# Clustered attention and a SoLU block on one core: another order of all queues, and small copies, casts, scalings and products shared otherwise between three engines

## The chip, the cores and the metric

The kernel runs on one core of a Trainium2 chip. The time is that of one execution on the device in microseconds (us); it is given as the median of several runs, and beside it stands one more execution that was taken with the hardware profiler. The engines are TensorE (PE in the profile, its weight loads PEld), VectorE (DVE), ScalarE (ACT), GpSimd (POOL) and SyncE (SP, which issues most DMAs). Each engine works through its own queue in the order in which its instructions were written, and waits at an instruction until what it needs is there.

## The reference

Attention for 4 batches, 8 heads, 768 tokens and 64 columns, in which a query sees the keys of its own cluster alone (16 clusters for each head, chosen by the greatest product with a normalised centroid), and behind it a block with two weights over the 3072 tokens:

```python
q_assign = np.argmax(np.einsum('bhsd,hcd->bhsc', q_n, c_n), axis=-1)
k_assign = np.argmax(np.einsum('bhsd,hcd->bhsc', k_n, c_n), axis=-1)
scores = np.where(q_assign[..., :, None] == k_assign[..., None, :], scale * q @ k.T, -1e9)
attn = softmax(scores) @ v
x = attn.transpose(0, 2, 1, 3).reshape(B * S, H * D)      # 3072 x 512
h = x @ w_in                                              # 3072 x 1024
solu = h * softmax(h)
ln = (solu - mean) / sqrt(var + 1e-6) * g_ln
out = ln @ w_out                                          # 3072 x 512
```

## The kernel before, in words

The work is cut into named steps. A step is written with `add(name, engine, ..., fn, needs, after)`; its function emits the instructions. What sets the order is a list written out by hand or by a program, `ORDER`: `Weave.run` goes through it and calls one function after the other, so each engine's queue is the list's steps of that engine in the list's order. `AWAY` names the steps that run on another engine than their default. A step's numbers are batch, pair of heads, and so on.

*Loads and clusters.* `ld` and `lv` load q, k and v for a pair of heads. In the first batch PE turns the tokens (`tp`, L396), and two copies to SBUF take them up: `xa` and `xt` (L407 on ACT, L409 on DVE). In the later batches DVE turns them (`xt`, L421). `ca` casts them to bf16 into `qbig` and `kbig` (L437 on ACT, L439 and L441 on DVE or POOL); `cv` casts v (L554 on ACT, L556 on the others). `cl` are the products with the centroids (L470), which `cx`, `cy`, `cz`, `cp` and `cb` have normalised, turned and written into `g_wide` (`cb` is L934). Then DVE turns the result back (`tb`, L479), takes the maximum (`mx`, L489), compares (`oh`, L493) and turns the one-hot rows (`ot`, L505 or L500). `pl` copies them below the casted q and k (L529 on ACT, L531 on the others), so that the product of the scores holds the mask; `bl` clears unused rows.

*Attention.* `S` are scores (L641), in regions of 1024 columns; four banks, `sb0` and `sb1`, hold two regions in turn. `E` is the exponential of a region on ACT (L651, 144 of them), which can start when both its halves are there, and frees the region for the scores two further on. `V` are the products with v (L663) into the one bank `ob`; `N` (L675, L686) divides by the sum on DVE and frees `ob` for the next group. In the first batch the heads come in the order of the pairs: pair 0 has the first nine regions, pairs 1 to 3 three each.

*The block.* `tx` turns x by DMA; `h` is the product with w_in (L774) into the banks `hb0` and `hb1`; `hm` (L784, DVE) brings it to SBUF and takes the maximum; `ex` (L800, ACT) is the exponential; `u` the product of both (L807, POOL or DVE); `tu` turns u by DMA (the last two by PE, L761, and a copy); `bn`, `ag` and `as` (DVE, POOL) and `al` (L842, POOL) make the variance and the factor alpha; `y` is the product with w_out (L846); `sc` scales it by alpha (L859 on ACT, L861 on DVE) and `ou` writes it out. There are 24 blocks of 128 tokens. Up to the 21st all y go through the one bank `mb`, so y of a block starts when `sc` of the block before has read the bank. `ce` (L618 on DVE, L622 and L624 on POOL) centres w_out once, `wi` casts w_in.

So the choice of an engine is made by lines such as these, and nothing else in the steps knows of it:

```python
def on(name, engine):
    return AWAY.get(name, engine)
...
e = on(f"sc{f}", "ACT")
```

## Time and profile before

| | us |
|---|---|
| median of 3 runs | 222.06 |
| the three runs | 222.46, 222.06, 220.9 |
| the profiled execution | 221.02 |
| its span, first to last instruction | 219.2 |
| busy: PE, ACT, DVE, POOL | 211.8, 193.0, 185.0, 159.0 |

The profile's page gives an engine's busy time as a share of the span; a share near one says that the engine is worth a look, not that it is the bound everywhere. The stages (a table of stretches of time) tell where each engine is full. In the groups of instructions the last columns are the busy time, the mean of one in ns, and the idle time of the engine just before them with what ended it. In a timeline each row has its start, its duration, the engine, the line and the operation.

### The profile page before, as it was taken

What the parts mean: (1) busy time and instruction counts of PE and PEld (TensorE: products, weight loads), DVE (VectorE), ACT (ScalarE), POOL (GpSimd) and SP (SyncE); (2) the same over time, 40 slices, a digit from 0 to 9 for tenths busy, and PEclk for the clock granted to TensorE, in tenths of its full rate; (3) what the DMA queues carried; (4) which work ended last, traced back from release to release, by engine and by line L of the source; (5) the groups of instructions that cost most, each with busy time, mean ns of one, the idle gap of its engine ahead of it and who ended that gap; (6) DMA issues with size and microseconds to landing.
All of it is one profiled execution on the core that took longest, in us unless ns stands there. A gap on an engine that the chain in (4) does not pass through costs nothing.

```text
span 219.2 us, 6308 instructions
## 1 busy us (share of the span) xinstructions
PE 211.8 (97%) x2429; PEld 148.0 (68%) x2429; DVE 185.0 (84%) x429; ACT 193.0 (88%) x246; POOL 159.0 (73%) x198
## 2 busy tenths in 40 slices
PE   7799999999999999999999999999999999999993
PEld 3467477677678776777677677666677766755552
DVE  3699978978999999896899999994888756889893
ACT  4699999999999998999999989999999888785472
POOL 4586969987898999549939987979969154555530
PEclk9999999999999999999999999999999999999999
DMA  6999999999799992998989973939484329695614
GB/s 198 372 403 299 180 182 301 150 155 274 134 189 175 164 185 45 174 250 174 190 211 173 180 155 63 178 96 215 133 162 101 93 48 171 138 151 132 185 60 156
DMA packets 120910, 38.33 MB, mean 175 GB/s; under 512 B 109992, under 2 KB 116400, under 8 KB 120880
## 3 DMA queue, kind: packets, MB, share of 16 engines
q1 hardware_dynamic: 120448, 37.40, 81.1%
q10 hardware_dynamic: 432, 0.52, 0.7%
q8 instruction: 19, 0.31, 0.6%
q14 instruction: 11, 0.09, 0.2%
HBM read 23.11 MB, written 6.29 MB: 134 GB/s over the span
## 4 chain that ended last, share of the span: by engine, by line
PE 74%; ACT 10%; DVE 9%; issue 2%; DMA 2%; POOL 0%; SPq 0%; DVEq 0%
PE sb L641 22%; PE hb L774 17%; PE mb L846 15%; PE ob L663 12%; ACT e L651 7%; PE hb L470 3%; DMA raw<-in_k_dram 2%; DVE w_st L784 2%; DVE xt L421 2%; DVE bs L818 2%; PE hb L846 2%; ACT xt L407 1%; PE hb L396 1%; DVE x L686 1%; ACT v L554 1%
## 5 line engine op out<-in xcount | busy, mean ns | idle before, releaser
L651 ACT ACTIVATE e<-sb 128x1024 bf16<-128x1024 f32 x144 | 139.8, 1023 | 8.7 <-PE sb L641 7.9
L641 PE MATMUL sb<-qbig,kbig 80*128 80x256 bf16 (+3 forms) x648 | 83.7, 261 | 1.1 <-ACT e L651 1.0
L641 PEld LDWEIGHTS <-kbig 80*128 80x128 bf16 (+1 forms) x648 | 62.9, 119 | 25.5 <-issue 8.8
L807 POOL TENSOR_TENSOR u<-e_sb,w_st 128x1024 bf16<-128x1024 bf16 x21 | 45.0, 2144 | 19.3 <-ACT e_sb L800 13.1
L663 PEld LDWEIGHTS <-e 128*128 128x128 bf16 x1152 | 48.6, 97 | 10.4 <-DVE x L686 0.6
L774 PE MATMUL hb<-w_in_sb,xT 128*128 128x512 bf16 x192 | 53.4, 379 | 0.0
L663 PE MATMUL ob<-v,e 128*128 128x65 bf16 x1140 | 51.4, 193 | 0.0
L846 PE MATMUL mb<-w_out_c,uT 128*128 128x512 bf16 x168 | 45.6, 379 | 0.4 <-DVE y L861 0.4
L818 DVE BATCH_NORM_STATS2 bs<-u 128x6 f32<-128x512 bf16 x48 | 31.9, 681 | 1.1 <-POOL u L807 1.1
L800 ACT ACTIVATE e_sb<-w_st,nmax 128x1024 bf16<-128x1024 f32 (+1 forms) x25 | 27.8, 1113 | 5.5 <-DVE w_st L784 4.1
L441 POOL TENSOR_SCALAR kbig<-xt 64x768 bf16<-64x768 f32 (+1 forms) x32 | 28.4, 890 | 2.3 <-DVE xt L409 0.7
L439 POOL CAST qbig<-xt 64x768 bf16<-64x768 f32 (+1 forms) x31 | 25.0, 807 | 5.9 <-PE ob L663 2.7
L842 POOL TENSOR_TENSOR alpha<-var,halves 128x1 f32<-128x1 f32 x24 | 15.4, 643 | 11.7 <-DVE var L825 11.0
L421 DVE STREAM_TRANSPOSE xt<-raw 128x768 f32<-128x768 f32 x24 | 22.5, 959 | 0.1
L846 PEld LDWEIGHTS <-uT 128*128 128x128 bf16 x176 | 15.1, 97 | 9.8 <-issue 0.5
L774 PEld LDWEIGHTS <-xT 128*128 128x128 bf16 x192 | 15.8, 98 | 8.3
L686 DVE TENSOR_TENSOR x<-ob,den 128x256 bf16<-128x256 f32 (+2 forms) x40 | 19.0, 474 | 1.4
L784 DVE TENSOR_SCALAR_CACHE_REDUCE w_st<-hb 128x512 f32<-128x512 f32 x24 | 16.3, 681 | 4.0 <-PE hb L774 3.9
L784 DVE TENSOR_SCALAR_CACHE_REDUCE w_st<-hb,nmax 128x512 f32<-128x512 f32 x24 | 17.8, 742 | 2.1 <-PE hb L774 1.5
L675 DVE RECIPROCAL den<-ob 128x4 f32<-128x4 f32 (+2 forms) x40 | 7.1, 179 | 10.7 <-PE ob L663 10.4
L556 POOL CAST v<-vf 128x384 bf16<-128x384 f32 x22 | 11.7, 542 | 4.2 <-DMA vf<-in_v_dram 3.6
L531 POOL COPY kbig<-oht 32x768 f32<-32x768 f32 (+2 forms) x14 | 9.9, 711 | 3.2 <-DVE oht L505 1.3
(112 smaller groups left out, 201.4 us busy)
## 6 DMA issues: line engine op xcount, KB each, us to landing
vf<-in_v_dram SPq DMA_DIRECT2D x16, 384.0 KB, 5.7
out_dram<-y SPq DMA_DIRECT2D x20, 256.0 KB, 2.7
raw<-in_k_dram SPq DMA_DIRECT2D x26, 192.0 KB, 4.4
raw<-in_q_dram SPq DMA_DIRECT2D x24, 192.0 KB, 5.3
w_g<-in_moe_w_out_dram SPq DMA_DIRECT2D x4, 512.0 KB, 8.6
w_st<-in_moe_w_in_dram SPq DMA_DIRECT2D x4, 512.0 KB, 7.1
raw<-in_q_dram SPq DMA_DIRECT2D x3, 384.0 KB, 6.5
raw<-in_k_dram SPq DMA_DIRECT2D x3, 384.0 KB, 7.6
```

The lines of the kernel that those rows point to most:

```text
L421: nc.vector.transpose(xts[b, p, i][:], raw_of(b, p, i))
L439: (nc.vector if e == "DVE" else nc.gpsimd).tensor_copy(dst, src)
L441: (nc.vector if e == "DVE" else nc.gpsimd).tensor_scalar(dst, src, scalar1=inv_C, scalar2=1.0, op0=Alu.mult, op1=Alu.mult)
L641: nc.tensor.matmul(reg[:, c:c + wd], kb[u, pp, side_of(h), keys], qb[u, pp, side_of(h), su * P:su * P + wd])
L651: nc.scalar.activation(es[r][:, :w], src, Act.Exp, scale=exp_scale, bias=-exp_scale)
L663: nc.tensor.matmul(ops_of(group_of[n])[:, s, :VW], es[r][:, c0:c0 + P], v1[index[b, pair_of(h)] % R][:, side_of(h), kt, :VW], start=(kt == ...
L774: nc.tensor.matmul(hb[f2][:], xTs[f][:, dc, :], w_in_sb[:, dc, f2 * BANK:(f2 + 1) * BANK], start=(dc == 0), stop=(dc == n_dc - 1))
L784: nc.vector.tensor_scalar(ff[f, "h"][:, f2 * BANK:(f2 + 1) * BANK], hb[f2][:], scalar1=-1.0, scalar2=nmax[:, f2 - 1:f2] if f2 else 3.0e38, ...
L800: nc.scalar.activation(ff[f, "e"][:, cols(f, f2)], ff[f, "h"][:, cols(f, f2)], Act.Exp, bias=ff[f, "nmax"][:, n_ff2 - 1:], scale=-1.0, acc ...
L807: (nc.vector if e == "DVE" else nc.gpsimd).tensor_tensor(ff[f, "u"][:, cols(f, f2)], ff[f, "e"][:, cols(f, f2)], ff[f, "h"][:, cols(f, f2) ...
L818: nc.vector.bn_stats(ff[f, "bs"][:, f2, :], ff[f, "u"][:, f2 * BANK:(f2 + 1) * BANK])
L846: nc.tensor.matmul(y_of(f, x), ff[f, "uT"][:, fc, :], w_out_c[:, fc, parts_of(f, x)], start=(fc == 0), stop=(fc == n_fc - 1))
```

## The change

The two tables are exchanged: `ORDER` as a whole, and `AWAY`. The steps, their instructions and their conditions stay. The diff shows the whole of `AWAY`; of `ORDER` the first line stands for the rest.

```diff
 AWAY = {}
 AWAY.update(dict.fromkeys("""
-    tu22.1 ca0.0.1.1.0 ca0.2.0.1 ca1.0.0.1 ca3.1.1.0 ca3.2.0.1 cv0.0.1 cv0.1.0 cv0.2.1 cv1.2.0
-    cv1.3.1 cv2.0.1 cv2.1.0 cv3.0.0 cv3.0.1 cv3.3.0 pl0.0.0.1 pl0.0.1.0 pl0.1.1.1 pl2.2.1.0
-    xa0.0.0 xa0.1.0 xa0.1.1 xa0.2.0 xa0.2.1 xa0.3.0 xt0.1.0 xt0.1.1 xt0.2.0 xt0.3.0
+    cv0.1.0 cv1.0.1 cv1.2.0 cv2.2.1 pl0.0.0.0 pl0.0.1.0.0 pl3.2.1.1 tu22.1 xa0.0.1 xa0.1.0 xa0.1.1
+    xa0.2.0 xt0.1.0 xt0.1.1 xt0.2.0 xt0.2.1
 """.split(), "ACT"))
 AWAY.update(dict.fromkeys("""
-    as0 as11 as14 as15 as17 as18 as19 as2 as22 as23 as4 as5 as9 bl1.2 bl3.0 ce0 ce2 ce4 km mk
-    pl0.0.1.0.0 pl0.1.0.0 pl0.1.0.1 pl0.2.0.0 pl0.2.1.0 pl0.3.0.0 pl0.3.1.1 pl1.0.0.0
-    pl1.2.0.0 pl2.0.0.0 pl2.0.0.1 pl2.0.1.1 pl2.2.0.0 pl3.0.0.1 pl3.2.0.1 pl3.2.1.0 sc0 sc1
-    sc12 sc13 sc14 sc16 sc4 sc9
+    as1 as10 as14 as16 as18 as2 as20 as21 as22 as23 as3 as4 as7 bl2.0 ca0.0.1.0.0 ca0.2.1.1
+    ca0.3.0.0 ce0 ce2 ce4 cv0.0.0 km mk pl0.0.1.1.0 pl0.2.1.1 pl0.3.0.0 pl0.3.0.1 pl0.3.1.0
+    pl1.0.0.0 pl1.2.0.0 pl2.0.0.0 pl2.2.0.0 pl3.2.0.1 sc0 sc1 sc10 sc11 sc12 sc16 sc2 sc20 sc22 sc3
+    sc4 sc5 sc6 sc8 sc9 xt0.0.0
 """.split(), "DVE"))
 AWAY.update(dict.fromkeys("""
-    ca0.0.0.0.0 ca0.0.0.0.1 ca0.0.0.1.0 ca0.0.0.1.1 ce1 ce3 pl0.0.1.1 u0.0 u1.0 u10.0 u11.0
-    u12.0 u13.0 u15.0 u16.0 u17.0 u18.0 u19.0 u2.0 u21.0 u22.0 u3.0 u4.0 u5.0 u6.0 u7.0 u8.0
-    u9.0
+    ca0.0.0.0.0 ca0.0.0.1.0 ca0.0.0.1.1 ce3 pl0.0.0.1 pl0.0.1.0.1 pl0.0.1.1.1 u0.0 u1.0 u10.0 u11.0
+    u13.0 u14.0 u15.0 u16.0 u17.0 u18.0 u2.0 u20.0 u21.0 u22.0 u23.0 u23.1 u3.0 u4.0 u5.0 u6.0 u7.0
+    u8.0 u9.0
 """.split(), "POOL"))
...
 ORDER = """
-lc ld0.0.0.0 ld0.0.1.0 ld0.0.0 ld0.0.1 ld0.1.0 ld0.1.1 lv0.0 ld0.2.0 ld0.2.1 ld0.3.0 lo3 lv0.1
+lc cx ld0.0.0.0 cy cz wu tp0.0.0.0 ld0.0.1.0 ld0.0.0 tp0.0.0.1 cp xa0.0.0 ld0.0.1 ld0.1.0 tp0.0.1.0
...
```

Counted over the program, ACT gives up seven `sc`, six `cv`, four `ca`, one `pl` and three copies of the first batch. DVE gets seven `sc` (15 in all), one `cv`, three `ca`, three copies of the first batch, one `ce`, and gives up seven `pl` and the two halves of the last `u`. POOL gets eight `pl`, five `cv` and those two halves. The changed kernel is two lines shorter, so its lines have numbers that are lower by two.

Three places of the queues follow. The first is ACT from its fifth exponential to the twelfth (before) and from the first to the tenth (changed): L651 and L649 are the exponentials, the other rows are copies and casts that stand between them. Before:

```order
L651 ACTIVATE e_370<-sb0_90 128x1024
L651 ACTIVATE e_372<-sb1_91 128x1024
L651 ACTIVATE e_427<-sb0_90 128x1024
L651 ACTIVATE e_429<-sb1_91 128x1024
L554 CAST v1_1_103<-vf_157 128x6x64
L529 COPY kbig0_99<-oht_374 32x384
L651 ACTIVATE e_482<-sb0_90 128x1024
L651 ACTIVATE e_484<-sb1_91 128x1024
L437 ACTIVATE qbig1_97<-xt_277 64x6x128
L651 ACTIVATE e_519<-sb0_90 128x1024
L554 CAST v1_2_104<-vf_161 128x6x64
L651 ACTIVATE e_526<-sb1_91 128x1024
```

Changed:

```order
L649 ACTIVATE e_278<-sb0_90 128x1024
L405 COPY xt_289<-hb1_93 128x384
L649 ACTIVATE e_306<-sb1_91 128x1024
L649 ACTIVATE e_314<-sb0_90 128x1024
L649 ACTIVATE e_337<-sb1_91 128x1024
L649 ACTIVATE e_375<-sb0_90 128x1024
L649 ACTIVATE e_396<-sb1_91 128x1024
L649 ACTIVATE e_403<-sb0_90 128x1024
L649 ACTIVATE e_436<-sb1_91 128x1024
L649 ACTIVATE e_453<-sb0_90 128x1024
L552 CAST v1_1_103<-vf_304 128x6x64
L649 ACTIVATE e_480<-sb1_91 128x1024
```

A copy and a cast are left between the exponentials of the first batch's start; the row of q's cast (L437), the one-hot copy (L529) and the second cast of v are on other engines now. Behind the last row shown the changed queue has exponentials alone until past the 21st.

The second place is DVE at the start, from the write of the centroids on (`cst` is the turned-back product, `oh` and `oht` the one-hot rows). Before:

```order
L409 COPY xt_195<-ob_94 128x3x2x64
L934 TENSOR_TENSOR g_wide_113<-mb_95,upper_136 128x256
L479 STREAM_TRANSPOSE cst_208<-mb_95 128x192
L489 TENSOR_REDUCE mx_210<-cst_208 128x12
L493 TENSOR_TENSOR oh_212<-cst_208,mx_210 128x192
L505 STREAM_TRANSPOSE oht_214<-oh_212 128x3x64 x2
L479 STREAM_TRANSPOSE cst_255<-mb_95 128x192
L489 TENSOR_REDUCE mx_257<-cst_255 128x12
```

Changed:

```order
L407 COPY xt_166<-hb0_92 128x3x2x64
L407 COPY xt_166<-hb1_93 128x3x2x64
L932 TENSOR_TENSOR g_wide_113<-mb_95,upper_136 128x256
L439 TENSOR_SCALAR kbig0_99<-xt_186 64x2x3x64
L477 STREAM_TRANSPOSE cst_201<-mb_95 128x192
L487 TENSOR_REDUCE mx_211<-cst_201 128x12
L491 TENSOR_TENSOR oh_214<-cst_201,mx_211 128x192
L477 STREAM_TRANSPOSE cst_222<-mb_95 128x192
L487 TENSOR_REDUCE mx_225<-cst_222 128x12
L503 STREAM_TRANSPOSE oht_227<-oh_214 128x3x64 x2
```

DVE has q's two copies and one cast of k more there, and the second half's turn and maximum stand before the first half's one-hot turn. On PE, at the same time, the turn of the next pair's tokens that stood before the first cluster products stands behind them.

The third place is DVE late in the program, around the scalings of y (`y<-mb,alpha`). Before:

```order
L818 BN_STATS bs_3352<-u_3322 128x6
L675 RECIPROCAL den_3354<-ob_94 128x4
L686 TENSOR_TENSOR x_2909<-ob_94,den_3354 128x256
L784 TENSOR_SCALAR w_st_3357,nmax_3358<-hb0_92 128x512
L861 TENSOR_SCALAR y_3368<-mb_95,alpha_3366 128x512
L818 BN_STATS bs_3352<-u_3322 128x6
L675 RECIPROCAL den_3435<-ob_94 128x4
L686 TENSOR_TENSOR x_2909<-ob_94,den_3435 128x256
L784 TENSOR_SCALAR w_st_3357,nmax_3358<-hb1_93,nmax_3358 128x512
L861 TENSOR_SCALAR y_3479<-mb_95,alpha_3433 128x512
```

Changed:

```order
L859 TENSOR_SCALAR y_3327<-mb_95,alpha_3096 128x512
L782 TENSOR_SCALAR w_st_3370,nmax_3371<-hb0_92 128x512
L782 TENSOR_SCALAR w_st_3370,nmax_3371<-hb1_93,nmax_3371 128x512
L821 BN_AGGR mv_3378<-bs_3184 128x2
L823 TENSOR_SCALAR var_3380<-es6_3314,esum_3055,mv_3378 128x1
L816 BN_STATS bs_3384<-u_3144 128x6 x2
L821 BN_AGGR mv_3410<-bs_3384 128x2
L823 TENSOR_SCALAR var_3412<-es6_3367,esum_3066,mv_3410 128x1
L835 TENSOR_SCALAR es6_3414<-esum_3204 128x1
L859 TENSOR_SCALAR y_3442<-mb_95,alpha_3168 128x512
L816 BN_STATS bs_3461<-u_3250 128x6
```

Between two scalings there stand now two maxima and two statistics in a row, and the scalings of the ninth to thirteenth blocks are all on DVE, as are seven before them.

More of the change, by code (lines that the diff above doesn't have):

```diff
@@ new lines @@
+xt0.1.1 pl0.0.0.0 oh0.0.1 pl0.0.1.0 ot0.0.1 pl0.0.1.1 pl0.0.0.1 tp0.2.0.0 tp0.2.0.1 xa0.2.0
+pl0.0.1.0.1 cl0.1 cv0.0.1 ld1.0.0.0 xt0.2.0 pl0.0.1.0.0 ca0.0.0.1.1 pl0.0.1.1.1 ca0.1.0.0 S0.0 S0.1
+ca0.1.1.0 tp0.2.1.0 ca0.2.0.0 pl0.0.1.1.0 E0 tp0.2.1.1 S1.0 ca0.2.0.1 tb0.1 cv0.0.0 xa0.2.1 S1.1
+tp0.3.0.0 ca0.1.0.1 S2.0 S2.1 mx0.1 xt0.2.1 lv0.1 E1 cl0.2 S3.0 E2 oh0.1 S3.1 V0.0 xa0.3.0
+ca0.2.1.0 lo2 tp0.3.0.1 S4.0 S4.1 E3 ld1.0.0.1 V0.1 lo3 ot0.1 tp0.3.1.0 z1 ca0.1.1.1 S5.0 tb0.2
+S5.1 lv0.2 pl0.1.1.0 V1.0 mx0.2 gt pl0.1.0.1 xt0.3.0 E4 oh0.2 xa0.3.1 V1.1 S6.0 S6.1 N0 gk E5
@@ L142 @@
+ag23 ptu23.1 tu23.1 al23 y22.2 y22.3 tu23.0 sc21 y23.0.0 y23.1.0 ou20 y23.1.1 sc22 ou21 y23.1.2
+y23.1.3 ou22 y23.0.1 y23.0.2 y23.0.3 sc23.1 sc23.0 ou23.1 ou23.0
 """.split()
```

195 lines of the change are left out of this document (93 added, 102 removed).

## The prediction

> **What bounds the kernel now.** I read the page first, then the stages, then the chain of waits, then the groups of one stage at a time. The page's busy times, and its shares of the chain that ended last:
>
> ```profile
> PE 211.8 (97%) x2429; PEld 148.0 (68%) x2429; DVE 185.0 (84%) x429; ACT 193.0 (88%) x246; POOL 159.0 (73%) x198
> PE 74%; ACT 10%; DVE 9%; issue 2%; DMA 2%; POOL 0%; SPq 0%; DVEq 0%
> ```
>
> TensorE (PE) is busy nearly always and is three quarters of the chain. That is an average, and the stages differ. The columns here are the stretch and its length, then the busy time of PE, PE's weight loads, VectorE (DVE), ScalarE (ACT) and GpSimd (POOL):
>
> ```profile
> 0.00:12.20 12.20, 9.55 (x63) 5.03 (x64) 6.57 (x25) 7.14 (x15) 6.46 (x26) 1.00 0.86 297
> 12.20:35.40 23.20, 22.10 (x286) 16.06 (x285) 20.10 (x45) 22.80 (x29) 18.37 (x30) 1.00 1.02 256
> 35.40:60.00 24.60, 24.60 (x334) 17.62 (x331) 22.32 (x46) 24.26 (x28) 21.26 (x25) 1.00 0.96 198
> ```
>
> From 35 us on PE has no idle time; from 12.2 to 35.4 ACT is busy 22.80 of 23.20 us. The chain of waits names the exponentials (L651) in that stage, one each 0.9 us, from 28.36 to 33.79 without a break:
>
> ```profile
> 28.36 0.81 ACT e L651
> 29.26 0.82 ACT e L651
> ...
> 33.79 1.09 ACT e L651
> ```
>
> How much PE can still win later is told by the groups of 35.4 to 216 us (busy, mean ns of one, then idle before):
>
> ```profile
> L641 PE MATMUL sb<-qbig,kbig 80*128 80x256 bf16 (+3 forms) x562 | 71.1, 259 | 0.0
> L846 PE MATMUL mb<-w_out_c,uT 128*128 128x512 bf16 x168 | 45.6, 379 | 0.4 <-DVE y L861 0.4
> ```
>
> One wait of 0.4 us in 180. So there are three stages: a start of 12 us (a chain of small steps), 23 us bound by ACT, and 180 us bound by PE, whose products stay what they are. Work taken off ACT can pay in the second stage alone; in the third the change can hardly win, and can lose.
>
> **Start.** The rows on the way to the first scores (L641) and the first exponential:
>
> ```profile
> 6.88 0.42 DVE L934 TENSOR_TENSOR g_wide<-mb,upper 128x256 f32<-128x256 f32 x1 [0.77 <-PE mb L931]
> 7.28 0.52 PE L396 MATMUL hb<-ident_f,raw 128*128 128x128 f32 x3 [0.44 <-ACT xt L407]
> 7.73 0.53 PE L470 MATMUL mb<-xt,g_wide 128*32 128x192 f32 x8
> 8.33 0.38 DVE L479 STREAM_TRANSPOSE cst<-mb 128x192 f32<-128x192 f32 x1 [1.02 <-PE mb L470]
> 9.53 0.64 DVE L505 STREAM_TRANSPOSE oht<-oh 128x192 bf16<-128x192 bf16 x2
> 11.45 0.35 ACT L529 COPY kbig<-oht 32x192 f32<-32x192 f32 x1
> 12.25 0.60 PE L641 MATMUL sb<-qbig,kbig 80*128 80x256 bf16 x4
> 12.89 1.02 ACT L651 ACTIVATE e<-sb 128x1024 bf16<-128x1024 f32 x1
> ```
>
> In the old order a turn of tokens (7.28) stands before the first cluster products (7.73). In the new one the products come first and can start when L934 has written the centroids, at about 7.1: two copies now stand before it on DVE, which idled 0.77 us there. That is 0.6 us sooner, so the turn back (8.33) comes at 7.7. Then DVE's own steps: turn, maximum and comparison of the first half 1.2 (8.33 to 9.53); turn and maximum of the second, now before L505, two thirds of that, 0.8; L505 0.64; comparison and L505 of the second half 0.4 + 0.64; one copy, 0.35 as at 11.45. The last one-hot rows lie at 11.6 to 11.8, which is where they are now (11.45 + 0.35), but PE was then behind them by 0.45 and a turn of tokens has left that place. First exponential 0.3 to 0.6 us sooner; I take 0.5.
>
> **ACT up to the 21st exponential.** ACT's groups of 12.2 to 35.4 us:
>
> ```profile
> L651 ACT ACTIVATE e<-sb 128x1024 bf16<-128x1024 f32 x21 | 20.1, 1038 | 0.1
> L407 ACT COPY xt<-hb 128x384 f32<-128x384 f32 x4 | 1.9, 484 | 0.2 <-PE hb L396 0.2
> L554 ACT CAST v<-vf 128x384 bf16<-128x384 f32 x2 | 1.0, 511 | 0.0
> L437 ACT ACTIVATE qbig<-xt 64x768 bf16<-64x768 f32 x1 | 0.8, 842 | 0.0
> L529 ACT COPY kbig<-oht 32x384 f32<-32x384 f32 x1 | 0.5, 507 | 0.0
> ```
>
> Two of the four L407 stand before the first exponential. Behind it: 2 x 0.48 + 2 x 0.51 + 0.84 + 0.51 = 3.3 us that are no exponentials. The new queue has one L407 and one L554 there, 1.0 us. That is 2.3 us less, some 0.1 of it in ends that overlap the next start; I take 2.2. With the start, 2.7 us.
>
> **What DVE and POOL take over.** DVE was busy 20.10 of those 23.20 us. It now has two more copies like L409, a cast of v, two casts of tokens and one more L618 there, and a turn of the next batch's tokens (L421) stands earlier; two 32x192 and two 32x384 copies leave it. The rows:
>
> ```profile
> L409 DVE COPY xt<-hb 128x384 f32<-128x384 f32 x3 | 1.6, 550 | 0.1
> L531 DVE COPY qbig<-oht 32x384 f32<-32x384 f32 x4 | 2.2, 558 | 0.1
> L531 DVE COPY qbig<-oht 32x192 f32<-32x192 f32 x2 | 0.9, 452 | 0.0
> L618 DVE SCALAR_TENSOR_TENSOR w_out_c<-w_g,g_ln,y 128x512 bf16<-128x512 f32 x2 | 1.9, 934 | 0.0
> L421 DVE STREAM_TRANSPOSE xt<-raw 128x768 f32<-128x768 f32 x1 | 1.0, 967 | 0.0
> L439 POOL CAST qbig<-xt 64x768 bf16<-64x768 f32 x27 | 23.0, 852 | 5.0 <-PE ob L663 2.7 <-PE sb L641 1.1 <-ACT xt L407 0.4
> ```
>
> A cast of this kind on DVE is in no row: its bounds are the 32x192 copy (0.45) and POOL's cast (0.85). I take 0.6, nearer to the copies of the same engine. Sum: 2 x 0.55 + 3 x 0.6 + 0.9 + 1.0 - 2 x 0.45 - 2 x 0.56 = 2.8 us more, in a stage that is to become 2.7 us shorter: 22.9 us of work for 20.5. All of that does not fit. DVE's normalisations free the bank `ob`; the values that wait for it hold PE's queue, and with it the scores behind them. How much of the 2.4 us is only the overlap of one instruction's end with the next one's start, these rows don't tell; if none of it is, 0.3 us of the gain is left, and if two thirds are, 1.9. At the upper end the casts cost 0.45 each and all 2.7 passes. Between ends so far apart I take **1.9**, since the row it rests on (L651 in a full queue: 1.04 us long, one each 0.9) shows such an overlap of a seventh. POOL was idle 4.8 us in the stage; it gets three copies and loses two casts there: nothing.
>
> ```profile
> 48.82 1.16 DVE L531 COPY qbig<-oht 32x768 f32<-32x768 f32 x1
> 42.56 2.54 POOL L441 TENSOR_SCALAR kbig<-xt 64x768 bf16<-64x768 f32 x2
> ```
>
> These are copies and casts that took far longer than others of their kind: 1.16 where the 32x384 copy takes 0.56, and 1.27 each where POOL's cast takes 0.85. Both engines were at work in both places. The Trainium skill has a rule that speaks against the change here: the GPSIMD Engine Reference, 1. Specifications, says that GpSimd shares its SBUF interfaces with VectorE and contends with Vector instructions in a 2-port mode or with two SBUF inputs. By it the work moved off ACT, which is not named there, would slow both of the others (the second rival); by the group means, which have such rows in them already, it is priced above.
>
> **PE's 180 us.** ACT gives seven scalings of y to DVE: no gain, since ACT is not the limit. The possible loss is in the order. y goes through one bank, `mb`, so y of the next block of tokens waits for the scaling of this one:
>
> ```profile
> 85.60 0.59 PE L846 MATMUL mb<-w_out_c,uT 128*128 128x512 bf16 x2 [0.35 <-DVE y L861]
> 199.56 0.60 PE L846 MATMUL mb<-w_out_c,uT 128*128 128x512 bf16 x2
> 200.30 0.67 ACT L859 ACTIVATE y<-mb,alpha 128x512 f32<-128x512 f32 x1
> 41.96 0.86 PE hb L774 x4
> 43.36 0.55 PE ob L663 x18
> 43.91 0.44 PE sb L641 x4
> ```
>
> From the start of a y's last pair of products to the end of its scaling are 1.41 us (199.56 to 200.97); 0.43 of it is PE's own (half of L774's 0.86), so some 1.0 us of other products must lie between one y and the next. Counted by the last three rows (0.43 for a pair at L774, 0.18 for six at L663, 0.22 for two at L641), the old order leaves at least 1.1; the new one leaves 0.9 to 1.3 at eight places after the ninth y, three of them scaled on DVE. Each may lose nothing, or 0.4 as at 85.60: 0 to 3.2 us. I take **0.5**.
>
> **The end.** Both halves of the last u go from DVE to POOL:
>
> ```profile
> 210.22 1.34 DVE L807 TENSOR_TENSOR u<-e_sb,w_st 128x512 bf16<-128x512 bf16 x2
> 212.48 0.61 PE L761 MATMUL sb<-ident_b,u 128*128 128x128 bf16 x8
> 206.27 2.14 POOL L807 TENSOR_TENSOR u<-e_sb,w_st 128x1024 bf16<-128x1024 bf16 x1 [1.74 <-issue]
> ```
>
> On POOL the two halves take the 2.14 of a whole one, until 212.36 instead of 211.56. Their turn by PE starts at 212.48, behind products of the two blocks before, which are the cover; without it the step costs 0.8. I take 0.
>
> **Sum.** -1.9 + 0.5 = -1.4 us. The profiled execution took 221.02 us (span 219.2), so 219.6 by its measure; the median of the three runs is 222.06, 1.04 above it, so 220.7 by that one. I name the middle, **220.1**.
>
> **Rivals.** 1: DVE has room, and no y waits. For it: two thirds of DVE's excess may be overlap, and closer pairs of y (1.1) cost nothing at 199.56. All 2.7 pay: 218.3 by the profiled run, 218.8 by the middle. 2: DVE takes ACT's place as the bound of the first 35 us, with POOL's contention. For it: 22.9 us of work for 20.5, and five moved copies that lose 0.6 as at 48.82 would add 3.0. Against: DVE's mean for such a copy, 0.56, says that few do. Time: no change, 221.0 to 222.1. 3, slower: DVE's scalings hold PE in the stage where PE is the bound. Fifteen now go through DVE's queue; where one finds a single instruction of 0.7 ahead of it, the bank is late by as much. With three that late the 1.9 is gone; with eight, 5.6 - 1.9 = +3.7, so 224.7 by the profiled run. For it: 85.60. Against: eight scalings were DVE's already, and one of them shows a wait. 4: the order changes nothing because PE is the bound throughout; against it stands the second stage's row.
>
> **How the numbers follow.** My sum has 0.38, rival 1 0.30, rivals 2 and 4 together 0.17, rival 3 0.15. About 1% (2.2 us) is what a measurement of this kernel can tell from no change; the three runs shown lie 0.7% apart. Nearly all of rival 1 and three tenths of my own case (a better cap, no loss at y) are past it: faster 0.40. The rest of mine with rivals 2 and 4: same 0.45. Slower 0.15. The range reaches from all 2.7 with 1.3 us of further waits won in the first 35 us (217.0) to rival 3 with four late scalings beside the median (222.06 + 2.8 - 1.9 = 223.0).
>
> **What would show it.** Right: the first exponential at 12.3 to 12.6 us; the 21st at 32.7 to 33.5 instead of 34.9 (33.79 + 1.09); DVE idle under 1.5 us in the second stage; then PE without idle to the end but for single waits of its y products for DVE's scalings. Wrong: the 21st exponential after 34.5 (DVE or contention took the place), more than 2 us of waits of PE for scalings, or PE waiting for the last u.

## The result, and the profile after

The change makes the kernel slower: 230.05 and 230.34 us, beside 220.72 to 222.46 for the kernel before on the same chip, a ratio of 1.038 with a 95% interval of 1.033 to 1.044. (Two more executions, 234.06 and 948.26 us, fell in a disturbed state and are left out.) The prediction said 220.1, with a range to 223.0; it was wrong in sign. The profiled execution took 230.05 us with a span of 228.2, so 9.0 us more span than before (219.2). The page, its busy times and its chain:

```profile
PE 214.8 (94%) x2399; PEld 147.9 (65%) x2429; DVE 192.3 (84%) x434; ACT 183.4 (80%) x225; POOL 167.5 (73%) x213
PE 58%; DVE 16%; POOL 14%; issue 6%; ACT 4%; DMA 1%; POOLq 0%; DVEq 0%; ACTq 0%
```

ACT gave up 9.6 us of work, as the change says, DVE took up 7.3 and POOL 8.5. The chain tells more: PE's share went from 74% to 58%, and POOL, which was not on the chain at all, has 14%, DVE 16% instead of 9%. The second of the stages shown for the kernel before, and a later stretch:

```profile
12.20:35.40 23.20, 21.85 (x280) 14.74 (x273) 22.09 (x47) 20.40 (x25) 19.55 (x36) 1.00 1.05 249
140.00:170.00 30.00, 26.79 (x316) 18.82 (x318) 24.74 (x52) 24.51 (x30) 25.52 (x30) 1.00 0.39 84
```

The later stretch in the kernel before:

```profile
140.00:170.00 30.00, 30.00 (x329) 21.14 (x324) 24.36 (x59) 28.77 (x39) 25.54 (x28) 1.00 0.73 137
```

In the second stage ACT is no longer full (20.40 of 23.20, was 22.80), and DVE is (22.09, was 20.10). From 140 to 170 us PE, which had no idle time, idles 3.2 us. What it waited for, over the whole changed kernel (line waited for, us in total, times, longest):

```profile
PE hb L772 <- DVE w_st L782: 2.0, 1, 2.0
PE ob L661 <- DVE x L684: 1.8, 2, 1.0
...
PE sb L844 <- DVE w_g L766: 1.1, 1, 1.1
```

Four waits, 4.9 us, all for DVE and none for a scaling of y (one of 1.2 us at the very start, left out here, is in both kernels). They end at 70, 156, 161 and 223 us, and the chain of waits goes through DVE ahead of each. DVE from 147 to 161 us, in the order of its queue, with rows left out:

```profile
147.76 0.56 DVE L684 TENSOR_TENSOR x<-ob,den 128x384 bf16<-128x384 f32 x1
148.23 2.75 DVE L491 TENSOR_TENSOR oh<-cst,mx 128x768 bf16<-128x768 f32 x1
...
155.44 0.56 DVE L684 TENSOR_TENSOR x<-ob,den 128x384 bf16<-128x384 f32 x1
...
156.63 3.07 DVE L529 COPY qbig<-oht 32x768 f32<-32x768 f32 x1
...
160.38 0.74 DVE L782 TENSOR_SCALAR_CACHE_REDUCE w_st<-hb,nmax 128x512 f32<-128x512 f32 x1
```

and POOL at the same time:

```profile
148.03 2.13 POOL L805 TENSOR_TENSOR u<-e_sb,w_st 128x1024 bf16<-128x1024 bf16 x1
...
156.35 0.82 POOL L439 TENSOR_SCALAR kbig<-xt 64x768 bf16<-64x768 f32 x1
157.15 2.13 POOL L805 TENSOR_TENSOR u<-e_sb,w_st 128x1024 bf16<-128x1024 bf16 x1
```

A comparison that takes 0.95 us elsewhere took 2.75: it began 0.20 us behind a u and ended at 150.98, 0.82 us behind u's end (150.16). A one-hot copy took 3.07 us beside a cast and the next u, and ended 0.42 us behind that u. The normalisation at 155.44 and the maximum at 160.38 stood behind these two in DVE's queue, and PE's `V` and `h` waited for them. At 64 and 219 us the same is seen, again a u on POOL beside a comparison, and beside the sum of the two halves' totals (`as` of the last block):

```profile
65.51 2.29 DVE L491 TENSOR_TENSOR oh<-cst,mx 128x768 bf16<-128x768 f32 x1
...
219.69 1.08 DVE L832 TENSOR_TENSOR es<-esum 128x1 f32<-128x1 f32 x1
```

```profile
64.52 2.46 POOL L805 TENSOR_TENSOR u<-e_sb,w_st 128x1024 bf16<-128x1024 bf16 x1
...
218.48 2.28 POOL L805 TENSOR_TENSOR u<-e_sb,w_st 128x512 bf16<-128x512 bf16 x2 [0.91 <-POOL alpha L840]
```

The view of one line's forms gives the spread (duration in ns: least, median, most), after:

```profile
L491 DVE TENSOR_TENSOR oh<-cst,mx x11: 317/950/2747, 8.9 to 148.2; 128x768 bf16<-128x768 f32 x6, 128x384 bf16<-128x384 f32 x3, 128x192 bf16<-128x192 f32 x2
```

and before:

```profile
L493 DVE TENSOR_TENSOR oh<-cst,mx x11: 359/948/1553, 9.1 to 146.9; 128x768 bf16<-128x768 f32 x6, 128x384 bf16<-128x384 f32 x3, 128x192 bf16<-128x192 f32 x2
L834 DVE TENSOR_TENSOR es<-esum x1: 143/143/143, 213.2 to 213.2; 128x1 f32<-128x1 f32 x1
```

Laid beside POOL's rows one by one, no comparison, no SBUF copy and no such sum of DVE ran beside a u in the kernel before. In the changed one five did that became longer by it: 1.3 (65.51), 0.4 (90.01), 1.8 (148.23), 2.5 (156.63; 0.55 elsewhere) and 0.9 us (219.69), some 7 us of DVE in all. Against this stands what the kernel before lost already: six of its comparisons and copies stood beside casts or copies on POOL (at 23.49, 48.82, 62.10, 87.08, 90.71 and 128.96) and were 0.4 to 0.7 us longer each, 3.4 us in all. So meetings are not new; new in the change is that they are with u, and so longer. DVE's statistics, maxima, turns, scalings and normalisations ran beside u dozens of times in both, with no change of length.

The first 36 us cost the rest that has a clear place. The first exponential started at 13.40 instead of 12.89, and the 20th ended at 36.18 instead of 34.88. (The prediction called that row the 21st; it is the 20th.) In the kernel before, the chain of waits of this stage went through ACT, from one exponential to the next. In the changed one it goes through POOL's queue alone, from 14.47 to 31.88 us:

```profile
14.47 0.25 POOL qbig L437
...
31.36 0.51 POOL kbig L529
...
31.92 0.41 PE sb L639 x2
```

Scores stood there behind casts and one-hot copies of POOL, and ACT waited for scores (2.6 us in six waits).

### The profile page after: what moved, and what is told of

Read it like the earlier page. It is cut to its first block, busy times and chain, and to the rows that moved or that the text cites. A ratio compares the mean times of both kernels' runs of the same rounds, so it can differ in the third digit from the quotient of the medians.

```text
span 228.2 us, 6282 instructions
## 1 busy us (share of the span) xinstructions
PE 214.8 (94%) x2399; PEld 147.9 (65%) x2429; DVE 192.3 (84%) x434; ACT 183.4 (80%) x225; POOL 167.5 (73%) x213
## 4 chain that ended last, share of the span: by engine, by line
PE 58%; DVE 16%; POOL 14%; issue 6%; ACT 4%; DMA 1%; POOLq 0%; DVEq 0%; ACTq 0%
PE sb L639 17%; PE mb L844 12%; PE hb L772 12%; PE ob L661 9%; ACT e L649 4%; PE hb L468 3%; POOL qbig L437 3%; DVE oh L491 3%; POOL kbig L439 3%; DVE bs L816 2%; DVE w_st L782 2%; POOL kbig L529 2%; POOL u L805 2%; POOL qbig L529 2%; POOL v L554 1%
## 5 line engine op out<-in xcount | busy, mean ns | idle before, releaser
L649 ACT ACTIVATE e<-sb 128x1024 bf16<-128x1024 f32 x144 | 141.1, 1022 | 21.9 <-PE sb L639 20.8
L639 PE MATMUL sb<-qbig,kbig 80*128 80x256 bf16 (+3 forms) x648 | 94.4, 263 | 2.2 <-ACT e L649 0.9
L639 PEld LDWEIGHTS <-kbig 80*128 80x128 bf16 (+1 forms) x648 | 61.4, 121 | 29.8 <-issue 10.4
L805 POOL TENSOR_TENSOR u<-e_sb,w_st 128x1024 bf16<-128x1024 bf16 (+1 forms) x23 | 47.6, 2071 | 24.3 <-DMA uT<-u 14.2
L661 PEld LDWEIGHTS <-e 128*128 128x128 bf16 x1152 | 50.4, 97 | 14.4 <-DVE x L684 3.9
L661 PE MATMUL ob<-v,e 128*128 128x65 bf16 x1140 | 54.2, 194 | 2.1 <-DVE x L684 1.8
L772 PE MATMUL hb<-w_in_sb,xT 128*128 128x512 bf16 x175 | 51.3, 379 | 2.6 <-DVE w_st L782 2.0
L844 PE MATMUL mb<-w_out_c,uT 128*128 128x512 bf16 x156 | 43.0, 379 | 0.4
L437 POOL CAST qbig<-xt 64x768 bf16<-64x768 f32 (+1 forms) x32 | 26.7, 839 | 2.9 <-DVE xt L407 1.8
L529 POOL COPY kbig<-oht 32x768 f32<-32x768 f32 (+2 forms) x17 | 13.1, 768 | 11.0 <-DVE oht L498 7.8
L554 POOL CAST v<-vf 128x384 bf16<-128x384 f32 x27 | 13.5, 515 | 0.7
```

Source lines behind the costliest of these rows:

```text
L437: (nc.vector if e == "DVE" else nc.gpsimd).tensor_copy(dst, src)
L639: nc.tensor.matmul(reg[:, c:c + wd], kb[u, pp, side_of(h), keys], qb[u, pp, side_of(h), su * P:su * P + wd])
L649: nc.scalar.activation(es[r][:, :w], src, Act.Exp, scale=exp_scale, bias=-exp_scale)
L661: nc.tensor.matmul(ops_of(group_of[n])[:, s, :VW], es[r][:, c0:c0 + P], v1[index[b, pair_of(h)] % R][:, side_of(h), kt, :VW], start=(kt == ...
L772: nc.tensor.matmul(hb[f2][:], xTs[f][:, dc, :], w_in_sb[:, dc, f2 * BANK:(f2 + 1) * BANK], start=(dc == 0), stop=(dc == n_dc - 1))
L805: (nc.vector if e == "DVE" else nc.gpsimd).tensor_tensor(ff[f, "u"][:, cols(f, f2)], ff[f, "e"][:, cols(f, f2)], ff[f, "h"][:, cols(f, f2) ...
```

## The experiments

The theory after the traces: (a) DVE's instructions with two operands in SBUF, and its copies from SBUF to SBUF, wait for the end of a POOL instruction that is under way; (b) in the first batch POOL's queue took ACT's place. The rivals: the moved work is the loss wherever it stands; or DVE is late by its order and the long rows fill time in which it would wait anyway. Each kernel's lines have the numbers of the kernel before. Medians in us and ratios to the kernel before:

| kernel | median | ratio, 95% interval |
|---|---|---|
| old order, new sharing | 252.4 | 1.139, 1.132 to 1.146 |
| new order, old sharing | 241.0 | 1.083, 1.074 to 1.092 |
| first 36 us old | 230.2 | 1.039, 1.033 to 1.045 |
| three steps off the meetings | 227.0 | 1.026, 1.020 to 1.031 |
| and POOL relieved in the first batch | 225.7 | 1.020, 1.016 to 1.024 |
| two u later | 228.3 | 1.030, 1.026 to 1.035 |
| before, last u on POOL | 221.5 | 1.001, 0.997 to 1.004 |
| all edits together | 225.1 | 1.015, 1.011 to 1.020 |
| the same, PE's holes filled | 224.7 | 1.012, 1.010 to 1.015 |
| new start, old rest | 222.8 | 1.007, 1.004 to 1.009 |
| new until 143 us, old end | 228.1 | 1.032, 1.028 to 1.035 |
| old until 145 us, new end | 231.8 | 1.048, 1.043 to 1.053 |

**Order and sharing apart.**

```diff
-ORDER of the change, AWAY of the change
+ORDER of the kernel before, AWAY of the change
```

> The old order with the new sharing between the engines. The theory: the new kernel loses its 9 us in two ways, in POOL's full queue in the first 36 us (some 1.5 us) and, for the larger part, where a comparison, an SBUF copy or the small sum of two numbers on VectorE stands beside a product u on GpSimd and waits for its end (2.75 us instead of 0.95, 3.07 instead of 0.65, 2.29 instead of 0.95, 1.08 instead of about 0.14). Which of these meet u depends on the order and on who makes u; with the old order the comparisons meet u at no place unless the moved u (the 14th-, 20th- and 23rd-block ones on GpSimd now) do, so I expect 223 to 226: the last u on GpSimd costs about 1 us, the rest a little. Rival: the moved work itself (scalings to VectorE, copies to GpSimd) is the loss whatever the order, then 228 to 231.

```diff
-ORDER of the change, AWAY of the change
+ORDER of the change, AWAY of the kernel before
```

> The new order with the old sharing. The theory: the meetings of comparisons and copies on VectorE with u on GpSimd at 65, 148 and 157 us come from the order and stay, the end (last u back on VectorE) is as before, and POOL's queue in the first 36 us is lighter: 225 to 229, with single waits of TensorE over 1 us for VectorE between 140 and 170 us. Rival (the moved work is the loss): 221 to 223.

Both missed by far, 252.4 and 241.0 us. An order that was made for one sharing is a bad order for the other: in the first, PE waits 4.3 us for maxima on DVE, 2.4 for POOL's one-hot copies, 2.1 for a scaling and 2.0 for a cast. So these two don't divide the 9 us, and nothing follows on the rival.

**The first 36 us old.**

```diff
-ORDER and AWAY of the change
+ORDER and AWAY of the kernel before up to the scores of region 21, of the change behind
```

> The changed kernel whose first part, until the scores of the 22nd region (some 36 us), has the old order and the old sharing; behind it all is as in the change. The theory: the first part is worth the time by which the 20th exponential came later (36.18 against 34.88 us) and perhaps a little more behind it, so 1 to 2 us less than the change: 228.0 to 229.3. Rival: the first part loses all (late by 1.3 us there, and everything behind it falls into worse meetings): under 225. Other rival: the later stages have slack for it, no change, 230.

230.2 us: no change. That is the time of the second rival, by which the later stages have slack; the theory missed. The trace doesn't settle it. Its first exponential started at 13.23 and the 20th ended at 35.59, so 0.6 us were won there, in spite of a new wait of 0.7 us for a load of w_out at 23 us; a second new wait, of 0.6 us for a normalisation at 36.8, stands at the seam, where eight steps of the new order are added, and took as much back. The four runs lie between 228.9 and 231.5, so one us can't be told here. The comparison of 2.74 and the copy of 3.07 us stand as in the change.

**Three steps off the meetings.**

```diff
 AWAY of the change, with
-u10.0 on POOL, pl3.2.0.1 and as23 on DVE
+u10.0 on DVE, pl3.2.0.1 on ACT, as23 on POOL
```

> The changed kernel with three steps on another engine: the product u of the eleventh block on VectorE instead of GpSimd (it stood beside the comparison that took 2.75 us), one copy of one-hot rows (the one that took 3.07 us beside the next u) on ScalarE instead of VectorE, and the two small operations of the last block's variance (1.08 us beside the last u, 0.14 elsewhere) on GpSimd instead of VectorE. The theory: TensorE's waits of 1.13 and 2.19 us at 156 and 161 us and most of the 1.22 us at 223 us go, so 225.5 to 227. Rival: VectorE's queue is late there because of its order, and the two long rows only fill time in which it would wait anyway: then 229 to 231, the waits of 1 to 2 us stay.

227.0 us, at the upper end of the theory's range and 3.2 us less than the change; the rival's 229 to 231 is out. DVE did not get less work of its own by it: u takes 1.22 us there, the copy and the sum that left take 0.55 and 0.14 by themselves. PE's waits:

```profile
PE ob L663 <- DVE x L686: 1.8, 2, 0.9
...
PE sb L846 <- DVE w_g L768: 0.5, 1, 0.5
```

The 2.0 us for the maximum are gone, the 1.1 at the end are 0.5. The wait for the normalisation at 155 us stayed (0.9): u itself on DVE now fills 1.22 us of the same queue. The two profiled executions differ by 4.1 us (230.05 and 225.98). PE's waits are 2.6 us of that; another 1.3 us are the start, whose first exponential came at 12.11 instead of 13.40 although nothing was edited there. So a part of the 3.2 us between the medians may be the start too.

**POOL relieved in the first batch.** The kernel just shown, and

```diff
-ca0.2.0.1, pl0.1.1.1, cv0.2.1 on POOL
+ca0.2.0.1, pl0.1.1.1, cv0.2.1 on ACT
```

> As the kernel with three steps moved (the one that took 226.97 us), and three more of the first batch go from GpSimd to ScalarE: one cast of q, one copy of one-hot rows and one cast of v, which were ScalarE's in the kernel before. The theory: behind the first exponential the changed kernel was bound by GpSimd's queue (no idle time from 12.9 to 32.9 us), since the 20th exponential ended 22.8 us after the start of the first one, against 22.0 before. With 1.9 us less on GpSimd that stretch becomes 21.3 to 22.0 us, and the time 0.7 to 1.5 us less: 225.5 to 226.3. Rival: ScalarE is the bound there after all; then the three steps make it 22.8 us or longer and the time stays at 227 or rises.

225.7 us, a time within the theory's range. But it is 0.5% below the kernel just shown (ratios of 1.020 and 1.026, measured on two chips), and the two intervals overlap. Twenty us from the first exponential on, in the kernel before, in the change and here:

```profile
12.89:32.89 20.00, 19.17 (x242) 13.50 (x241) 17.48 (x40) 19.83 (x26) 15.37 (x25) 1.00 1.02 252
```

```profile
13.40:33.40 20.00, 18.97 (x241) 12.79 (x240) 19.02 (x40) 17.53 (x20) 18.15 (x33) 1.00 1.06 231
```

```profile
11.89:31.89 20.00, 19.44 (x244) 13.30 (x243) 19.23 (x40) 19.31 (x23) 16.09 (x30) 1.00 1.08 252
```

In the change ACT (the fourth engine, 17.53) has 2.5 us to spare, and POOL (the fifth) has 33 instructions instead of 25, 2.8 us more. With three of them back on ACT, PE gets 0.5 us more done in the 20. The stretch from the first exponential to the end of the 20th, however, fell only from 22.78 to 22.43 us, not to 22.0: by then PE, DVE and ACT are all near full. What the trace does show is the place of the bound: with these three steps back on ACT the chain of waits from the first exponential to the 20th has no piece of POOL any more, it goes through PE and ACT.

**The last u alone**, in the kernel before:

```diff
-u23.0 u23.1 on DVE
+u23.0 u23.1 on POOL
```

> The kernel before with one edit: both halves of the last block's u on GpSimd instead of VectorE, as in the change. The theory: the small sum on VectorE that stands behind them in the queue waits for the second half's end, its row becomes 0.8 us or more longer, the last copy of turned u comes later, and TensorE waits 0.6 to 1.2 us for it before the last products: 0.6 to 1.2 us more than before, 221.9 to 222.5. My prediction (products of the two blocks before cover it): no change.

No change, 221.5 us: the theory's 0.6 to 1.2 us missed, and the prediction's "0" for that edit was right in the old order. There a statistic stands ahead of the small sum on DVE, which meets only the rest of u:

```profile
211.49 0.69 DVE L818 BATCH_NORM_STATS2 bs<-u 128x6 f32<-128x512 bf16 x1 [0.64 <-POOL u L807]
212.10 0.50 DVE L834 TENSOR_TENSOR es<-esum 128x1 f32<-128x1 f32 x1
```

So u on POOL is not enough for the 1.1 us at the end of the change; the sum right behind its start belongs to it (with that sum on POOL, three steps moved, the wait was 0.5).

**The meeting by itself.** Behind the last step of the kernel before, five kinds of DVE instruction run alone and behind the start of POOL's instructions; nothing else is at work. `step` is a tiny operation on one number for each row, by which one engine waits for the other; `hot`, `copy`, `small`, `stats` and `turned` are the comparison, the one-hot copy, the sum, the statistic and the turn of the kernel.

```diff
+for fn in (hot, copy, small, stats, turned):
+    for pool, k in ((one_u, 0), (one_u, 1), (one_u, 2), (one_cast, 1), (one_cast, 2)):
+        step(nc.gpsimd, 1, 0)
+        for _ in range(k):
+            pool()
+        step(nc.vector, 2, 1)
+        fn()
+        step(nc.vector, 0, 2)
```

> The kernel before with a measurement behind its last step, so its whole time says nothing: five kinds of VectorE instruction (a comparison, a copy of one-hot rows, the small sum of two numbers for each row, a statistic, a turn by VectorE) each run alone, behind the start of one u and of two in a row on GpSimd, and behind one and two casts there; at the end u is started behind the first three. The theory: alone 0.95, 0.55, 0.14, 0.68 and 0.97 us; behind one u the first three end after u does (about 1.9 us longer), the last two do not change; behind two u the three either wait for one (the engine behind gets its turn between two instructions) or for both (4 us longer), which the copy of 3.07 us suggests, since a cast and then a u ran beside it. Rival: both engines share and slow each other in part, then all five become longer by some tenths and u becomes longer than 2.14 us too.

DVE's rows; for each kind the first row is alone, the second behind one u, the third behind the first of two (a fourth, where shown, behind one cast):

```profile
223.13 0.95 DVE L1349 TENSOR_TENSOR oh<-cst,mx 128x768 bf16<-128x768 f32 x1
224.59 2.92 DVE L1349 TENSOR_TENSOR oh<-cst,mx 128x768 bf16<-128x768 f32 x1
228.03 2.92 DVE L1349 TENSOR_TENSOR oh<-cst,mx 128x768 bf16<-128x768 f32 x1
233.33 1.61 DVE L1349 TENSOR_TENSOR oh<-cst,mx 128x768 bf16<-128x768 f32 x1
...
238.24 0.55 DVE L531 COPY qbig<-oht 32x768 f32<-32x768 f32 x1
239.54 2.40 DVE L531 COPY qbig<-oht 32x768 f32<-32x768 f32 x1
...
251.60 0.15 DVE L1357 TENSOR_TENSOR gate<-esum 128x1 f32<-128x1 f32 x1
252.32 2.12 DVE L1357 TENSOR_TENSOR gate<-esum 128x1 f32<-128x1 f32 x1
...
263.07 0.68 DVE L1361 BATCH_NORM_STATS2 bs<-u 128x6 f32<-128x512 bf16 x1
264.26 0.69 DVE L1361 BATCH_NORM_STATS2 bs<-u 128x6 f32<-128x512 bf16 x1
...
274.72 0.97 DVE L1364 STREAM_TRANSPOSE oht<-oh 128x768 bf16<-128x768 bf16 x1
276.18 0.97 DVE L1364 STREAM_TRANSPOSE oht<-oh 128x768 bf16<-128x768 bf16 x1
```

and POOL's beside the second and the third of these rows:

```profile
224.57 2.13 POOL L1341 TENSOR_TENSOR u<-e_sb,w_st 128x1024 bf16<-128x1024 bf16 x1
228.01 4.94 POOL L1341 TENSOR_TENSOR u<-e_sb,w_st 128x1024 bf16<-128x1024 bf16 x2
```

The comparison that began at 224.59 ended at 227.51, 0.81 us behind the end of u (226.70); the copy 0.41 behind, the sum with it. The statistic and the turn did not notice u at all, and u beside one DVE instruction is not slowed: 2.13 us. So it is no sharing, it is waiting for the whole instruction, and theory (a) is shown for these kinds. Behind two u DVE got its turn between them (2.92 again), and the second u was the one that waited: the two took 4.94 instead of 4.3 us. (In a last part u was to start behind the three; its rows begin only when the DVE instruction it was meant for has ended, so that part says nothing.) The Trainium skill has this rule (SBUF — State Buffer, SBUF: two separate sides): the port pair that both engines use is a lock, held for the whole instruction by whichever started first. These rows agree with it.

That leaves the copy of 3.07 us, which waited for a cast and for the u behind it. A second measurement of the same build has chains made of casts and u:

```diff
+    for fn in (copy, hot):
+        for chain in ((one_cast, one_u), (one_u, one_cast), (one_cast, one_cast, one_u), (one_cast, one_u, one_u)):
+            for lead in (1, 2, 3):
...
```

> The kernel before with a second measurement behind its last step; its whole time says nothing. A copy of one-hot rows and a comparison on VectorE start 0.2 to 0.6 us into a chain on GpSimd: a cast and a u, a u and a cast, two casts and a u, a cast and two u. In the measurement before, VectorE's instruction got its turn behind one cast or one u, and the next one on GpSimd waited for it. In the changed kernel a copy that stood beside a cast and then a u took 3.07 us, as if it had waited for both. If the first holds always, the copy takes 0.5 to 1.1 us behind a cast and a u (2.4 behind a u); if GpSimd's next instruction can get in ahead, 2.6 to 3.3 us in some of the places.

```profile
225.48 3.01 DVE L531 COPY qbig<-oht 32x768 f32<-32x768 f32 x1
229.62 2.82 DVE L531 COPY qbig<-oht 32x768 f32<-32x768 f32 x1
233.20 2.40 DVE L531 COPY qbig<-oht 32x768 f32<-32x768 f32 x1
...
243.94 1.10 DVE L531 COPY qbig<-oht 32x768 f32<-32x768 f32 x1
```

The first two stand beside a cast and then a u and waited for both, the third beside a u and then a cast, the last beside two casts and then a u: these two waited for the first instruction alone. It was the same at every one of the three starting points (2.82 to 3.20 us beside a cast and a u), and for the comparison too (3.33 to 3.71). So a u that follows a cast at once gets in ahead of the DVE instruction that waits; a cast behind a u or behind a cast does not. Why is open.

**Two u later, and everything together.** The kernel with three steps moved, and

```diff
-u1.0 tu1 ahead of ca1.1.0.1, u10.0 on DVE
+u1.0 tu1 behind pl1.2.1.0, u10.0 on POOL behind pl3.2.1.0
```

> As the kernel with three steps moved (226.97 us), but two products u stay on GpSimd and are written later in its queue: the second block's behind the first one-hot copy of that batch's second half (so that VectorE's comparison, 2.29 us beside it, is over by then), the eleventh block's likewise (GpSimd instead of VectorE). The theory: the waits of TensorE of 1.03 us at 69 us and 1.08 us at 155 us, both for a normalisation on VectorE, go: 224.5 to 225.5. Rival: VectorE is late there by its own load, the waits stay, 226.5 to 227.5; or u comes too late for its turn and y waits, then over 228.

228.3 us, the time of the second rival; from 227.0 it is not clear of the spread of the runs, and in the profiled execution the first exponential came at 13.55, 1.4 us later than in the kernel with three steps moved. The comparison that took 2.29 us takes 0.97 and the waits at 69 and 155 us are gone. But the second block's u met another row in its new place: the one-hot copy at 69.94 took 2.08 us beside it. And u is late by then, and its followers are too:

```profile
PE ob L663 <- POOL v L556: 1.1, 1, 1.1
PE mb L846 <- DVE y L861: 0.9, 1, 0.9
```

The other way round, with u1.0 early, on the kernel with six steps moved:

```diff
-u1.0 behind ca1.1.1.1, u10.0 on DVE, bn23.1 ag23 ahead of tu23.1
+u1.0 behind ex1.0, u10.0 on POOL behind pl3.2.1.0, bn23.1 ag23 al23 behind tu23.1
```

> As the kernel that took 225.73 us (six steps moved), with four more edits: the eleventh block's u stays on GpSimd, behind the one-hot copy that follows the comparison it used to meet; the second block's u is written right behind the first block's, so that it is over before the comparison; and of the last block's statistics the second one and the last sums stand behind the copy of turned u on VectorE instead of ahead of it. The theory: the waits of 1.03 us (at 68 us), 1.08 us (154 us) and 0.62 us (218 us) go, so 223.0 to 223.8. Rival: as in the run where u came later, other waits take their place: 225 to 227.

225.1 us: missed by 1.3. All waits of PE for a normalisation and for the last copy are gone, and a new one of 1.0 us for a cast of q on POOL, now behind u1.0, has come at 63 us. These edits give 5.1 us back (230.2 to 225.1), of which up to 1.3 may be the start again: of the change there are two executions, and the profiled one started late. What is left, 1.5% over the kernel before, was not taken apart.

**The start.** PE's turns of tokens at 5.7 and 6.3 us took 0.85 us each in the profiled execution of the change, and 0.49 in others of the same order:

```profile
5.71 0.85 PE L394 MATMUL ob<-ident_f,raw 128*128 128x128 f32 x3
6.34 0.85 PE L394 MATMUL sb<-ident_f,raw 128*128 128x128 f32 x3
```

```profile
5.70 0.49 PE L396 MATMUL ob<-ident_f,raw 128*128 128x128 f32 x3
6.03 0.49 PE L396 MATMUL sb<-ident_f,raw 128*128 128x128 f32 x3
```

(the second is the kernel with six steps moved). To see whether PE's holes ahead of them matter:

```diff
             nc.tensor.transpose(turn_bank(p, i, hf)[:, j * P:(j + 1) * P],
                                 tokens_of(b, p, i)[:, hf, j * P:(j + 1) * P], ident_f[:])
+        if (b, p, i) == (0, 0, 0):
+            nc.tensor.matmul(sb[0][:, 0], idle[:, :P], idle)
```

> As the kernel of the same call with four more edits, and two products more on TensorE that write nothing of use (128x512, into a bank that is free), one behind each half of the first turn of tokens, in the holes of 0.6 and 0.7 us at 4.4 and 5.5 us. The theory: the turns of tokens at 5.7 to 10 us, which took 0.85 us each in some executions of the new order and 0.49 to 0.55 in others, are slow where TensorE had holes before them; with the holes filled they take 0.49 to 0.55, the first exponential starts at 12.0 to 12.3 us, and the runs lie closer together, at the lower end of those of the kernel beside it. Rival: the holes have nothing to do with it, the spread stays, and the two products cost 0 to 0.4 us.

The turns took 0.69 and 0.49, the first exponential started at 12.27, and the six runs lie within 223.96 to 224.89 instead of 224.03 to 226.45. That is what the theory expects, but the kernel beside it had its first exponential at 12.28 in the one execution profiled, so it is a hint and not shown. That one had turns of 0.85 and 0.76 us at 5.7 and 6.4 us, so slow turns there do not make a late start by themselves.

**The new start, and the two halves.** The change up to the first scores, the old kernel behind; the change until region 112, the old kernel behind; and the reverse:

```diff
-ORDER and AWAY of the kernel before
+ORDER and AWAY of the change up to the scores of region 1, of the kernel before behind
```

> The kernel before with the change's order and sharing until the first scores only (the first 12 to 13 us), the old ones behind. Where TensorE's turns of tokens took 0.49 to 0.55 us, the first exponential started at 11.9 to 12.3 us with the new start and at 12.3 to 13.2 with the old one, so the new start by itself is worth 0.5 us, as predicted: 220.6 to 221.3, faster than both kernels if that holds. Rival: the following steps of the old order wait for the same loads and copies as before, then no change, 221.4 to 221.9.

```diff
-ORDER and AWAY of the change
+ORDER and AWAY of the change up to the scores of region 112, of the kernel before behind
```

> The new order and sharing until the scores of region 112 (some 143 us), the old ones behind. If the two long waits at 156 and 161 us and the one at the end make up 5.0 of the 9 us, this has the other part alone: 3.0 to 4.5 us more than before, 224.5 to 226.0. If the end is late only because of what came before it (work pushed on from the middle), then it stays late: over 227.

```diff
-ORDER and AWAY of the change
+ORDER and AWAY of the kernel before up to the scores of region 112, of the change behind
```

> The old order and sharing until the scores of region 112 (some 145 us), the new ones behind: it has the comparison, the copy and the small sum that stand beside u at 148, 157 and 219 us of the change, and nothing else of it. 4 to 5.5 us more than before, 225.5 to 227. If the long waits need what came before them in the change, under 223.

222.8, 228.1 and 231.8 us; all three missed. The new start alone gains nothing, it loses 0.4 to 0.9%: its first exponential started at 12.30, yet the 20th ended at 35.36. The halves miss their ranges upwards, and the first lies in its rival's (over 227). The first has new waits behind its seam: 1.3 us for scalings on ACT and 1.1 for a maximum. In the second PE idles 1.8 us from 100 to 150 us, ahead of and at its seam, where the kernel before idles nothing, and it waits 1.7 us instead of 1.0 for the normalisation at 157. The losses (6.7 and 10.4 us) add up to more than 9, so the halves don't divide them either. One thing does follow from the last kernel. What came before 145 us is old, and the three late waits are there again:

```profile
PE hb L774 <- DVE w_st L784: 2.2, 2, 2.0
PE ob L663 <- DVE x L686: 1.7, 1, 1.7
...
PE sb L846 <- DVE w_g L768: 1.1, 1, 1.1
```

They stand on their own and are not pushed on from the middle.

## Why the prediction was wrong, point by point

**Start, -0.5.** The first exponential came 0.5 us later, not sooner. Over the profiled executions of all kernels but the two that join an order to another sharing, it started at 11.89, 12.11, 12.27, 12.28, 12.30, 13.40, 13.55 and 13.82 us with the new start, and at 12.28, 12.68, 12.89, 13.23, 13.88 and 15.22 with the old one. Executions with the same start lie up to 1.9 us apart, far more than the 0.5 that was predicted, so the step can't be called right or wrong from one trace, and the 0.5 us that the change lost here may be chance; and where it was sooner (the new start alone) the rest did not follow.

**ACT's relief, -2.2, capped to -1.9.** This step failed. ACT got its relief, 2.3 us in 20; the stretch from the first exponential to the end of the 20th became 22.78 us, from 21.99. The same stretch was 22.79 us with three steps moved, in an execution that started at 12.11, so it is the change's and not the start's. The sentence that failed is "it gets three copies and loses two casts there: nothing", about POOL. By its rows from 12 to 36 us POOL had 11 one-hot copies for 6, 6 casts of v for 5 and 11 casts of q and k for 12; in 20 us it had 33 instructions for 25. The bound went from ACT to POOL, whose queue is the chain from 14.47 to 31.88 us, and not to DVE, as the prediction feared (DVE was busy 22.09 of 23.20 us, and is not on that chain). Relieving POOL by three steps took it off the chain and made the stretch 0.4 us shorter. With the start, the prediction had the 20th exponential 1.9 us earlier; it ended 1.3 us later, and at 34.90, no earlier than before, in the execution that started at 12.11.

**DVE and POOL beside each other.** The step that cost most: its sum has no term for it. The prediction had found the two engines slowing each other, named it as a rival, and priced it at 0.6 us a copy, from the copy of 1.16 at 48.82, and held the group's mean, 0.56, against it. Neither row bounds it, and the mean was misread: its four rows took 0.35, 0.35, 1.01 and 0.52 us, so two of the four were longer already. What such an instruction loses is the rest of the POOL instruction that is under way: 0.6 beside a cast of 0.8, up to 2.5 beside a cast and a u. In the trace of before no such instruction stood beside a u, so neither a row nor a mean could show that price. Even so POOL's u of 2.14 us was quoted: an instruction that must wait for all of it loses about 2 us a meeting. DVE lost some 7 us in these meetings, and PE waited 4.9 for what stood behind them.

**y through `mb`, +0.5, and the third rival.** The tight pairs cost nothing: PE has no wait for a scaling in the changed kernel. The rival had the right engine, DVE, and the wrong place: PE was held by `hm` and `N`, whose banks `hb` and `ob` wait for DVE, not by `sc`.

**The end, 0.** It cost 1.1 us. The cover that was named (products of the two blocks before) did hide POOL's slower u, as the old order with that one edit shows, but for a wait of 0.4 us in its profiled execution and no change of the time. What came late was the copy of turned u, behind a sum on DVE that waited for u.

Together: the 20th exponential 1.3 us later and 4.9 us of waits for DVE are 6.2 of the 9.0 us, if they simply add up. The cause of the remaining 2.8 stays open: besides these, PE's recorded waits behind the 20th exponential are a single one of 0.3 us.

## What to carry to other kernels

Before work moves to GpSimd or to VectorE, lay the two new queues beside each other and look for VectorE instructions with two SBUF operands, or SBUF copies, that will stand beside a long GpSimd instruction: each of the kinds measured here costs what is left of that instruction (and of a product u that follows a cast at once), and the price is on VectorE's queue and on all that waits for it. A mean from a trace in which such a pair never stood together says nothing of it. Count a stage's work from its own queue in the new order, for each engine that takes something over, not from totals over the program; and don't join an order to a sharing that it was not made for.

## What the runs showed of the hardware that was not expected

- A VectorE instruction that waits for GpSimd gets its turn behind one u or one cast, but not when a u follows a cast at once: 2.82 to 3.20 us for the copy and 3.33 to 3.71 for the comparison, over three starting points.
- GpSimd waits just so for VectorE: a u behind a comparison that had got its turn took 2.73 us instead of 2.13.
- The first 10 us are not the same in all executions: TensorE's turns of tokens at 5.7 us take 0.49 or 0.85 us in the same kernel order, with a granted clock of 1.00 in the profile's rows in both, and the first exponential started anywhere from 11.89 to 13.82 us with the new start and from 12.28 to 15.22 with the old one. The Trainium skill (TensorE: Matmul & The Clock Gate, Part 1) has a gate that opens after about 3.4 us of work by a window that runs freely, so that it opens earlier or later from run to run; the two durations, a factor of 1.7 apart, would fit it, and the granted clock here does not show it.
- In the kernel with the old order and the new sharing, which idled PE most of all the whole kernels, the mean granted clock of the profiled execution was 0.955 instead of 1.00. In the two executions with a measurement behind the last step it was 0.53 and 0.52 over that measurement, in which PE has next to nothing to do.
